# The fifth pair's queries: a buffer freed by moving the first pair's rest, an earlier load, a later scaling

## The chip, the cores and the metric

The kernel runs on one core of a Trainium2 chip. The metric is the device time in microseconds. Before, six runs gave a median of 1515.28 us (1513.14 to 1515.76).

The engines are named as in the profile: PE is TensorE (matmuls; PEld are its weight loads), DVE is VectorE, ACT is ScalarE, POOL is GpSimd, SP is SyncE, whose queue here issues nearly all loads. Each engine works through its own queue in order and waits on semaphores for the others.

## The reference

An attention with a threshold, for 8 batches of 8 heads with 576 positions and a head size of 64, followed by a SwiGLU block over the 4608 tokens that come out of it:

```python
scores = scale * np.matmul(q, k.transpose(0, 1, 3, 2))       # scale = 1/8
thresh = np.max(scores, axis=-1, keepdims=True) - tau
scores = np.where(scores >= thresh, scores, -1000000000.0)
scores = scores - np.max(scores, axis=-1, keepdims=True)
attn = np.exp(scores)
attn = attn / (np.sum(attn, axis=-1, keepdims=True) + 1e-09)
attn_out = np.matmul(attn, v)                                # q, k, v: (8, 8, 576, 64)
x = attn_out.transpose(0, 2, 1, 3).reshape(8 * 576, 512)
g = x @ w_gate                                               # w_gate, w_val: (512, 1536)
silu = g * (1.0 / (1.0 + np.exp(-g)))
out = (silu * (x @ w_val)) @ w_out                           # w_out: (1536, 512)
```

All is in float32.

## The kernel before

**Pairs, tiles and segments.** Two heads make a pair; a batch has four pairs (NP = 4), the whole input 32. A pair's 576 queries are cut into four tiles of 128 and one of 64. Pair and tile numbers in the code count from 0: the "fifth pair" is pair 4, the first of the second batch. The main loop (L856 to L923) runs over segments. The first four segments are the first two tiles of pairs 0 to 3 (tiles one to eight of the run). The next four are the three remaining tiles of pairs 3, 0, 1 and 2 (tiles nine to twenty). From then on each segment is one whole pair in another layout ("halved"). In the loop `n` is the segment and `x` the tile in it, so `n == NP - 1` holds the seventh and the eighth tile, and `n == NP` begins with the ninth.

**One tile.** `scores` (L316) is a generator that a tile steps through: score matmuls on PE (L343, or L348 for the short tile), the row maximum on DVE (L370), threshold and exponential on ACT (L376, L377), masking with the row sum on DVE (L381), sum and reciprocal `ri` (L405, L406), and, from the third tile of a pair on, the division by the sum: the first head on ACT (L389), the second on POOL (L387). `flip` (L431) then turns the tile before on PE, one head after the other (L447; both scaled heads are needed), and ACT copies the two heads out of PSUM (L455) and the end piece (L460). `attend_tile` (L463) multiplies with the values (L475, L479), copied by ACT (L481). Between these steps `fill` issues matmuls of the SwiGLU block (`pg` and `pv`, L537) as far as rows of it are ready; the order of all this is written out by hand. The PSUM tiles of `flip`, `attend_tile` and the SwiGLU block share four buffers, so a new one waits for the copy out of an older one.

**Weights.** The weights come in pieces through a few places: two DMA issues on SP (L185), a split in two by ACT (L196, L197), three steps on DVE (L203, L207, L210) and a sum on POOL (L212). One piece goes through per tile; the load of the next into a place waits until the piece there is split and joined.

**Queries and keys.** `load_qk` (L231) loads a pair with four DMA issues for the keys and four for the queries. For pairs 1, 2 and 3 the raw data have places of their own in larger buffers (`places_`, L235); pair 0 and all pairs from 4 on use the tiles `qraw` and `kraw` of a pool with a single buffer each (L242). For pairs 0 to 3 the first 256 queries (QA) are loaded at once, and the remaining 320 later, by `load_rest` (L272), into the same raw tile; each load is followed by a scaling by `scl` on POOL (L253), which the main loop takes out of the deque `scales` at a tile of its choice (L914 to L920). From pair 4 on, `load_qk` issues eight loads on SP and the scaling of all 576 queries at once (L278 to L280). The loop calls it for the next pair in the first tile of each segment from the fifth on (L886), for pair 4 thus in the ninth tile.

**Transposes.** `prepare` (L804) turns a pair's raw keys and queries with DVE. The rests of pairs 0, 1 and 2 are turned in the ninth, tenth and eleventh tile (L902 to L904). Pair 0's rest is read there out of the very `qraw` that pair 4's queries take next, so pair 4's first load waits for that transpose.

`xall` holds the rows for the SwiGLU block (five parts of XW = 1024 columns, XB = 5) and behind them two parts of 768, `hs2` and `hs3`, used from the third unit of that block on. Pair 3's raw keys and queries lie in the first 1152 columns behind XB * XW.

Of the kernel before, what the change touches and what calls it, by code (L numbers as in the profile page):

```python
# [14 lines left out]
ALU = mybir.AluOpType  # L15
# [4 lines left out]
def kernel(  # L20
# [30 lines left out]
    nc = tc.nc  # L51
    P = 128
    B, H, S, D = q.shape
    NP = H // 2
# [3 lines left out]
    G = 32  # L58
    NG = P // G
    NJ = S // G  # L60
# [7 lines left out]
    XB = 5  # L68
# [5 lines left out]
    QA = TA * P  # L74
# [20 lines left out]
    scl = const.tile([P, 1], F32, name="scl")  # L95
# [21 lines left out]
    def run_idle(n):  # L117
        ps = ps_f.tile([P, 512], F32, name="idle", tag="psf")[:, 0:TC]
        for _ in range(n):
            nc.tensor.matmul(ps, ones[:, 0:P], ones, start=True, stop=True)  # L120
# [9 lines left out]
    XW, HW = NCC * TC, NF2 * P  # L130
    xall = const.tile([P, XB * XW + 2 * HW], F32, name="xall")
# [84 lines left out]
    def need(n):  # L216
        while len(joined) < n:
            fetch_weights(2)
            if not split:
                split_weights()  # L220
            join_weights()
            split_weights()
# [8 lines left out]
    def load_qk(i):  # L231
        b, hp_ = divmod(i, NP)
        tiles = {}

        places_ = {1: extra[:, 0:2 * S], 2: extra[:, 2 * S:4 * S], 3: xall[:, XB * XW:XB * XW + 2 * S]}  # L235
        srcs = {"q": (q, "(j r) (e d) -> e r j d"),
                "k": (k, "(j r) (e d) -> e r j d" if b == 0 else "(r j) (e d) -> e r j d")}
        for x, name in enumerate("qk"):
            if i in places_:
                tiles[name] = places_[i][:, x * S:(x + 1) * S].rearrange("p (j d) -> p j d", d=G)  # L240
            else:
                tiles[name] = ld.tile([P, NJ, G], F32, name=f"{name}raw")  # L242
        raws = [tiles[name].rearrange("p j d -> p (j d)") for name in "qk"]

        def load(name, js, queues):
            src, order = srcs[name]
            for g in range(NG):
                h, e = divmod(g, 2)
                queues[g // 2].dma_start(out=tiles[name][g * G:(g + 1) * G, js],
                                         in_=src[b, 2 * hp_ + h].rearrange(order, r=G, d=G)[e][:, js])  # L250

        def scale(cs):
            nc.gpsimd.tensor_scalar(out=raws[0][:, cs], in0=raws[0][:, cs], scalar1=scl, scalar2=None, op0=ALU.mult)  # L253

        if i < NP:

            queues = [nc.sync, nc.scalar if i < 2 else nc.sync]
            load("k", slice(0, NJ), queues)
            if i == 0:
                nc.scalar.dma_start(out=tau_s, in_=tau.partition_broadcast(P))  # L260
            load("q", slice(0, QA // G), queues)
            if i == 0:
                nc.vector.tensor_scalar(out=scl, in0=tau_s, scalar1=0.0, scalar2=SCALE, op0=ALU.is_ge, op1=ALU.mult)
                nc.vector.tensor_scalar(out=cap, in0=tau_s, scalar1=0.0, scalar2=2e38, op0=ALU.is_ge, op1=ALU.mult)
                nc.vector.tensor_scalar(out=cap, in0=cap, scalar1=-1e38, scalar2=None, op0=ALU.add)
                nc.vector.scalar_tensor_tensor(out=cut, in0=tau_s, scalar=-1.0, in1=cap, op0=ALU.mult, op1=ALU.min)
            elif i == 1:
                scale(slice(0, QA))
            else:
                scales.append(lambda: scale(slice(0, QA)))  # L270

            def load_rest():  # L272
                load("q", slice(QA // G, NJ), [nc.sync] * 2)
                scales.append(lambda: scale(slice(QA, S)))

            more_loads.append(load_rest)
        else:
            for name in "qk":  # L278
                load(name, slice(0, NJ), [nc.sync] * 2)
            scale(slice(0, S))  # L280
        return raws

    def load_v(seg):
# [446 lines left out]
    def fill(n):  # L730

        credit[0] += n
        while credit[0] > 0:
            c = next(pieces)
            left[0] -= c
            credit[0] = credit[0] - c if c else 0
            if not c:
                return 0
        return 1
# [18 lines left out]
    rest = list(range(TA, NT + 1))  # L758
# [36 lines left out]
    raws = {}  # L795
    more_loads, scales = deque(), deque()
    kept = {}
    later = []

    def fetch_qk(i):  # L800
        if i < NPAIR and i not in raws and i not in kept:
            raws[i] = load_qk(i)

    def prepare(seg):  # L804

        i = seg["i"]
        if i in kept:
            seg.update(kept[i])
            return
        qr, kr = raws[i]  # L810
        kept[i] = None
        qT = qkp.tile([P, S], F32, name="qT")
        if i < NP:
            kT = pall[:, 4 + i, :]
            rest = flat[:, i * (S - QA):(i + 1) * (S - QA)]
            nc.vector.transpose(out=kT, in_=kr)
            if i == 0:
                nc.vector.tensor_scalar(out=qr[:, 0:QA], in0=qr[:, 0:QA], scalar1=scl, scalar2=None, op0=ALU.mult)
            nc.vector.transpose(out=qT[:, 0:QA], in_=qr[:, 0:QA])

            later.append((rest, qr[:, QA:S]))
            if i == NP - 1:
                to, fr = later.pop()
                nc.vector.transpose(out=to, in_=fr)
            kept[i] = {"kT": kT, "qT": rest, "q0": QA}
        else:
            kT = qkp.tile([P, S], F32, name="kT")
            nc.vector.transpose(out=kT, in_=kr)
            nc.vector.transpose(out=qT, in_=qr)
        seg.update(kT=kT, qT=qT, q0=0)  # L830

    def give(n):
        for u in segs[n]["gives"]:
            ready.append(u)
            left[0] += cost(u)
        gains[n] = (gains[n][0], 0)

    run_idle(6)
    fetch_qk(0)
    prepare(segs[0])  # L840
    fetch_qk(1)

# [13 lines left out]
    for n, seg in enumerate(segs):  # L856
        if NP <= n < 2 * NP:
            seg["v"] = segs[seg["i"]]["v"]
        for x, t in enumerate(seg["tiles"]):
            go = scores(seg, t)  # L860
            next(go)
            if not n and not x:
                run_idle(6)
            next(last, None)
            attends = prev is not None and x == 1
            products = iter(())
            attend_tile()
            next(go)
            next(last, None)
            flip()  # L870
            if n == NP and x == 0:
                attend_tile()
                give(n - 1)
            if n == 2 * NP and x == 1:
                give(n - 1)
            if attends and n > 2 * NP:
                if prev["i"] % NP == 0:
                    need(NW)
                    start_batch(prev["i"] // NP)
                products = attend(prev)  # L880
            part = pace(n, x) / 2
            more = len(split)
            if n or x:
                split_weights()
                fetch_weights(2)
            if x == 0 and n >= NP:  # L886
                fetch_qk(seg["i"] + 1)
            next(go)
            double = t == NT and NP <= n < NP + 2
            if more and not double:  # L890
                join_weights()
            fill(part)
            next(go)
            fill(part)
            if double:

                join_weights(2)
                split_weights()
                fetch_weights(2)
            gates()  # L900
            last = go
            if n == NP and later:  # L902
                to, fr = later.pop(0)
                nc.vector.transpose(out=to, in_=fr)  # L904
            if attends and n > 2 * NP:
                next(products)
                next(products)
                give(n - 1)
            if attends and seg["halved"]:
                load_v(seg)  # L910
            if x == 0 and 0 < n < NP - 1:
                load_v(segs[n + 1])
                more_loads.popleft()()
            if n == 0 and x == 1 or n == 1:  # L914
                scales.popleft()()
            elif n == NP - 2 and x == 1:
                more_loads.popleft()()
                scales.popleft()()
            elif n == NP - 1:
                scales.popleft()()  # L920
            if x == len(seg["tiles"]) - 2 and n + 1 < len(segs):
                prepare(segs[n + 1])
        prev = seg  # L923
# [42 lines left out]
```

## Time and profile before

| | us |
|---|---|
| median of six runs | 1515.28 |
| lowest, highest run | 1513.14, 1515.76 |
| the profiled execution | 1514.41 |
| its span, first to last instruction | 1512.6 |
| PE busy in 75 to 160 us of the span | 81.23 of 85 |
| PE busy in 160 to 200 us | 33.11 of 40 |
| DVE busy in 160 to 200 us | 36.35 of 40 |
| PE busy in 200 to 1400 us | 1194.75 of 1200 |

The span is what one profiled execution shows from its first to its last instruction; the time of that execution lies 1.81 us above it. The change touches the stretch of the seventh to the eleventh tile, some 48 to 85 us after the start: the ninth tile's scores come at 53.4, the tenth's at 64.3, the eleventh's at 75.1. A list of waits tells which instruction stood idle for which other; a timeline gives each engine's instructions in order of time, with the idle time before one in brackets. PE's granted clock is shown per window; its mean over the span is 0.998.

### The profile page before, as it was taken

The numbers are of one execution on the slowest core, as the hardware profiler recorded it, in microseconds if no ns is written. First come the engines' busy times: TensorE is split into PE (matmuls) and PEld (weight loads), VectorE is DVE, ScalarE is ACT, GpSimd is POOL, SyncE is SP. The second block draws the span as 40 slices with busy tenths as digits, with TensorE's granted clock in tenths as the row PEclk, the third lists the DMA queues.
The fourth block names the chain that finished last, engine by engine and source line by source line (L and its number), as shares of the span: only waits on it lengthen the run. The fifth ranks groups of instructions, "written<-read, shape, count | busy, mean of one in ns | idle before, by whom it ended". The sixth has DMA issues, their size and how long they took to land. (4 is left out here: it accounts for less than half of the span.)

```text
span 1512.6 us, 31511 instructions
## 1 busy us (share of the span) xinstructions
PE 1485.2 (98%) x11808; PEld 1125.4 (74%) x11808; DVE 997.0 (66%) x3040; ACT 726.6 (48%) x2158; POOL 642.2 (42%) x640
## 2 busy tenths in 40 slices
PE   9899899999999999999999999999999999999998
PEld 6677564477777777787777777777777777888887
DVE  7878988777777777747667666776666767512212
ACT  6777665555455545434545445454544554311110
POOL 2545543367454535336444444543545353500000
PEclk9999999999999999999999999999999999999999
DMA  8642411211212111112111111112110120000000
GB/s 175 170 142 94 96 33 40 53 33 32 47 33 47 33 28 29 41 28 46 33 29 28 24 46 33 46 33 47 33 38 12 45 48 16 1 14 1 15 15 15
DMA packets 177064, 66.93 MB, mean 44 GB/s; under 512 B 159888, under 2 KB 159888, under 8 KB 176912
## 3 DMA queue, kind: packets, MB, share of 16 engines
q1 hardware_dynamic: 170880, 56.62, 16.4%
q0 software_dynamic: 2432, 7.87, 1.4%
q8 instruction: 94, 1.54, 0.4%
q10 hardware_dynamic: 3600, 0.43, 0.2%
q14 instruction: 58, 0.48, 0.1%
HBM read 55.44 MB, written 9.44 MB: 43 GB/s over the span
## 5 line engine op out<-in xcount | busy, mean ns | idle before, releaser
L387 POOL TENSOR_SCALAR pall<-pall,ri 128x288 f32<-128x288 f32 (+1 forms) x260 | 265.0, 1029 | 337.8 <-DVE ri L397 314.8
L537 PE MATMUL pv<-xall,wgv 128*128 128x256 f32 x1728 | 405.1, 383 | 1.6 <-ACT pall L455 1.3
L537 PE MATMUL pg<-xall,wgv 128*128 128x256 f32 x1728 | 403.6, 383 | 0.2 <-ACT pall L455 0.2
L537 PEld LDWEIGHTS pv<-xall,wgv 128*128 128x128 f32 x1728 | 324.8, 190 | 67.5 <-issue 22.3
L537 PEld LDWEIGHTS pg<-xall,wgv 128*128 128x128 f32 x1728 | 323.8, 190 | 65.5 <-issue 22.0
L358 DVE TENSOR_REDUCE mx<-sc 128x2 f32<-128x576 f32 x252 | 180.5, 751 | 237.6 <-PE sc L335 236.8
L381 DVE SCALAR_TENSOR_TENSOR pall<-sc,th,pall 128x288 f32<-128x288 f32 (+1 forms) x540 | 258.1, 528 | 31.1 <-ACT pall L377 31.1
L377 ACT ACTIVATE pall<-sc,nm 128x288 f32<-128x288 f32 (+1 forms) x540 | 236.4, 510 | 0.6
L373 ACT ACTIVATE th<-nm,cut 128x4 f32<-128x4 f32 (+1 forms) x140 | 41.6, 297 | 383.8 <-DVE nm L362 383.8
L569 POOL TENSOR_TENSOR ht<-ht,gt 128x512 f32<-128x512 f32 x84 | 107.0, 1274 | 194.0 <-DVE ht L557 109.8
L426 DVE STREAM_TRANSPOSE pall<-pall 128x576 f32<-128x576 f32 x252 | 181.4, 754 | 2.8 <-POOL pall L387 2.8
L635 PE MATMUL po<-wo,ht 128*128 128x256 f32 x768 | 177.5, 381 | 0.0
L335 PE MATMUL sc<-kT,qT 64*32 64x288 f32 x4032 | 158.5, 412 | 11.7 <-DVE pall L381 10.5
L635 PEld LDWEIGHTS po<-wo,ht 128*128 128x128 f32 x768 | 144.6, 190 | 26.4 <-issue 6.0
L557 DVE SCALAR_TENSOR_TENSOR ht<-tn,pv 128x512 f32<-128x512 f32 x102 | 69.9, 685 | 132.3 <-PE pv L537 119.1
L389 ACT ACTIVATE pall<-pall,ri 128x288 f32<-128x288 f32 (+1 forms) x264 | 132.9, 553 | 0.0
L311 ACT COPY sums<-sums 32x4 f32<-32x4 f32 (+1 forms) x560 | 108.4, 194 | 49.8 <-DVE pall L381 38.6
L550 ACT ACTIVATE tn<-pg 128x512 f32<-128x512 f32 x108 | 64.8, 600 | 139.8 <-PE pg L537 133.0
L501 PE MATMUL xa<-pall,vall 64*64 64x288 f32 x2016 | 128.7, 405 | 0.0
L335 PEld LDWEIGHTS sc<-kT,qT 64*32 64x32 f32 x4032 | 58.9, 106 | 89.4 <-issue 61.3
L501 PEld LDWEIGHTS xa<-pall,vall 64*64 64x64 f32 x2016 | 74.4, 133 | 50.7 <-ACT sums L311 3.6
L653 POOL TENSOR_TENSOR ht<-ht,xall 128x256 f32<-128x256 f32 x48 | 34.1, 729 | 156.3 <-PE po L635 155.1
(110 smaller groups left out, 1339.1 us busy)
## 6 DMA issues: line engine op xcount, KB each, us to landing
vall<-in_v_dram SPq DMA_DIRECT2D x112, 144.0 KB, 3.3
kraw<-in_k_dram SPq DMA_DIRECT2D x114, 72.0 KB, 2.7
qraw<-in_q_dram SPq DMA_DIRECT2D x112, 72.0 KB, 2.4
out_dram<-ob POOLq DMA_DIRECT2D x28, 256.0 KB, 2.6
wo<-in_moe_w_gate_dram SPq DMA_DIRECT2D x16, 384.0 KB, 3.6
wo<-in_moe_w_val_dram SPq DMA_DIRECT2D x16, 384.0 KB, 4.4
xall<-in_moe_w_out_dram SPq DMA_DIRECT2D x5, 768.0 KB, 4.6
wo<-in_moe_w_out_dram SPq DMA_DIRECT2D x3, 768.0 KB, 4.7
```

Of the source, the lines that this page charges most:

```text
L311: nc.scalar.copy(out, in_[:, :, 0])
L335: nc.tensor.matmul(ps[g * G:(g + 1) * G, h, 0:SH], qT[hs, col + a * G:col + (a + 1) * G], kT[hs, c * SH:(c + 1) * SH], start=True, stop=True)
L358: nc.vector.tensor_reduce(out=mx[:, 2 * x:2 * x + 2, 0], in_=tile_[:, :, 0:SH], axis=AX.X, op=ALU.max, negate=True)
L377: nc.scalar.activation(ps[x], scs[x], AF.Exp, bias=nm[:, x:x + 1])
L381: nc.vector.scalar_tensor_tensor(out=ps[x], in0=scs[x], scalar=th[:, x:x + 1], in1=ps[x], op0=ALU.is_ge, op1=ALU.mult, accum_out=sm[:, x, ...
L387: nc.gpsimd.tensor_scalar(out=ps[x], in0=ps[x], scalar1=ri[:, x:x + 1], scalar2=None, op0=ALU.mult)
L389: nc.scalar.activation(ps[x], ps[x], AF.Copy, scale=ri[:, x:x + 1])
L426: nc.vector.transpose(out=p, in_=p)
L501: nc.tensor.matmul(xa[a][h * D:(h + 1) * D, at:at + n * G].rearrange("d (i q) -> d i q", q=G), vr[rs, h, j, :], p[rs, lo:lo + n, j, :], st ...
L537: nc.tensor.matmul(ps[:, i], wgv[:, mat, c, (f + i) * P:(f + i + 1) * P], x[:, c, cs], start=(c == 0), stop=(c == NCC - 1))
L569: eng.tensor_tensor(out=hts[x], in0=hts[x], in1=gt, op=ALU.mult)
L635: nc.tensor.matmul(ps, h(f), w[:, f, :], start=(f == 0), stop=(f == NF2 - 1))
```

## The change

`load` gets an optional target, so that the rest of the queries can land elsewhere than in the raw tile; `scale` takes the data instead of a range of columns. Pair 0's rest gets 320 columns of `xall` behind pair 3's raw data (columns 1152 to 1472 behind XB * XW); the rests of the other pairs stay in their raw tiles. `raws[i]` gets a third entry, the rest, which `prepare` hands on to the transposes. Pair 4 no longer scales its queries where it loads them, but puts the scaling into `scales`. The load of pair 4 is called in the seventh tile (`n == NP - 1`; the second call in the eighth finds it done, as does the former call in the ninth), and the scaling is taken out in the tenth (`n == NP`, `x == 1`).

```diff
-        def load(name, js, queues):
+        def load(name, js, queues, to=None):
             src, order = srcs[name]
+            to = tiles[name][:, js] if to is None else to
             for g in range(NG):
                 h, e = divmod(g, 2)
-                queues[g // 2].dma_start(out=tiles[name][g * G:(g + 1) * G, js],
+                queues[g // 2].dma_start(out=to[g * G:(g + 1) * G],
                                          in_=src[b, 2 * hp_ + h].rearrange(order, r=G, d=G)[e][:, js])
 
-        def scale(cs):
-            nc.gpsimd.tensor_scalar(out=raws[0][:, cs], in0=raws[0][:, cs], scalar1=scl, scalar2=None, op0=ALU.mult)
+        def scale(x):
+            nc.gpsimd.tensor_scalar(out=x, in0=x, scalar1=scl, scalar2=None, op0=ALU.mult)
...
             elif i == 1:
-                scale(slice(0, QA))
+                scale(raws[0][:, 0:QA])
             else:
-                scales.append(lambda: scale(slice(0, QA)))
+                scales.append(lambda: scale(raws[0][:, 0:QA]))
+
+            own = xall[:, XB * XW + 2 * S:XB * XW + 3 * S - QA] if i == 0 else raws[0][:, QA:S]
+            raws.append(own)
 
             def load_rest():
-                load("q", slice(QA // G, NJ), [nc.sync] * 2)
-                scales.append(lambda: scale(slice(QA, S)))
+                load("q", slice(QA // G, NJ), [nc.sync] * 2, own.rearrange("p (j d) -> p j d", d=G))
+                scales.append(lambda: scale(own))
 
             more_loads.append(load_rest)
         else:
             for name in "qk":
                 load(name, slice(0, NJ), [nc.sync] * 2)
-            scale(slice(0, S))
+            if i == NP:
+                scales.append(lambda: scale(raws[0]))
+            else:
+                scale(raws[0])
         return raws
...
-        qr, kr = raws[i]
+        qr, kr = raws[i][0:2]
...
-            later.append((rest, qr[:, QA:S]))
+            later.append((rest, raws[i][2]))
...
             elif n == NP - 1:
                 scales.popleft()()
+                fetch_qk(NP)
+            elif n == NP and x == 1:
+                scales.popleft()()
             if x == len(seg["tiles"]) - 2 and n + 1 < len(segs):
                 prepare(segs[n + 1])
```

In the built program PE's and ACT's queues are the same instructions in the same order, and so is DVE's, but for the place from which it turns pair 0's rest. On SP the eight loads of pair 4 stand directly behind the weight piece of the seventh tile, ahead of two weight pieces that stood before them. On POOL pair 4's scaling stands behind the tenth tile's L212 instead of ahead of the ninth tile's L387.

## The prediction

> **What bounds the kernel now.** I read first the busy times of the page, for the engine whose work fills the span.
>
> ```profile
> PE 1485.2 (98%) x11808; PEld 1125.4 (74%) x11808; DVE 997.0 (66%) x3040; ACT 726.6 (48%) x2158; POOL 642.2 (42%) x640
> ```
>
> PE is busy for 1485.2 of 1512.6 us. The change neither adds nor removes a matmul, so it can win only out of the 27.4 us in which PE stands still, and out of time in which PE runs at a lower clock. The list of waits for the whole span has one large single wait of PE, 3.4 us, and the list for 60 to 80 us, which holds the stretch that the change touches, has what stands in front of it (columns: who waited for whom, total us, times, longest).
>
> ```profile
> POOL qraw L253 <- DMA qraw<-in_q_dram: 7.2, 1, 7.2
> ...
> PE tp L447 <- POOL pall L387: 3.4, 1, 3.4
> ```
>
> The timeline of each engine there (start us, duration, engine, line, work, then the idle time before it in brackets) gives the chain. DVE, SP, POOL and PE in this order:
>
> ```profile
> 61.68 0.51 DVE L904 STREAM_TRANSPOSE pall<-qraw 128x320 f32<-128x320 f32 x1
> ...
> 62.22 1.95 SPq L249 DMA_DIRECT2D qraw<-in_q_dram  x4
> 64.21 2.70 SPq L249 DMA_DIRECT2D kraw<-in_k_dram  x4
> 67.01 0.56 SPq L185 DMA_DIRECT2D wo<-in_moe_w_gate_dram  x1
> ...
> 57.97 1.08 POOL L253 TENSOR_SCALAR extra<-extra,scl 128x320 f32<-128x320 f32 x1
> 66.20 1.72 POOL L253 TENSOR_SCALAR qraw<-qraw,scl 128x576 f32<-128x576 f32 x1 [7.16 <-DMA qraw<-in_q_dram]
> 67.91 1.72 POOL L387 TENSOR_SCALAR pall<-pall,ri 128x576 f32<-128x576 f32 x1
> ...
> 65.62 0.66 PE L447 MATMUL tp<-pall 128*128 128x128 f32 x4
> 69.68 1.04 PE L447 MATMUL tp<-pall 128*128 128x128 f32 x4 [3.40 <-POOL pall L387]
> ...
> 71.58 3.57 PE L537 MATMUL pv<-xall,wgv 128*128 128x256 f32 x12
> 75.08 1.19 PE L348 MATMUL sc<-pall 64*64 64x288 f32 x8
> ```
>
> The fifth pair's queries land in the buffer that still holds the rest of the first pair's, so SP holds their load until DVE has transposed that rest (61.68 + 0.51 = 62.19). GpSimd's scaling of them stands in its queue ahead of the ninth tile's scaling (L387) and waits 7.16 us for the load; L387 ends at 69.6, and only then may PE turn the second head (L447). The last view is the windows: length, busy times by engine, then the granted clock (1.00 is full), DMA share, GB/s.
>
> ```profile
> 66.00:68.00 2.00, 0.28 (x3) 0.04 (x1) 1.67 (x3) 1.61 (x4) 1.79 (x2) 1.00 0.70 109
> 68.00:70.00 2.00, 0.32 (x2) 0.32 (x3) 1.93 (x7) 0.60 (x2) 2.00 (x2) 0.95 1.02 246
> 70.00:72.00 2.00, 2.00 (x8) 1.74 (x7) 1.97 (x2) 1.19 (x3) 2.00 (x2) 0.50 0.47 182
> 72.00:74.00 2.00, 2.00 (x8) 1.67 (x7) 1.92 (x3) 2.00 (x4) 2.00 (x2) 0.70 0.00 0
> 74.00:76.00 2.00, 2.00 (x14) 1.14 (x12) 0.00 (x0) 0.91 (x2) 1.50 (x1) 1.00 0.60 154
> ```
>
> After the stall PE gets half its clock: the missing shares 0.05, 0.50 and 0.30 of 2 us each, doubled, are 3.4 us at half rate. So the stall costs twice.
>
> **The change, part by part.**
>
> *Rest of the first pair's queries in a place of its own.* The four loads of 128x320, the 1.08 us scaling and the 0.51 us transpose stay, with the same sizes and at the same places in SP's, GpSimd's and DVE's queues; only the address differs. Cost 0. It frees the fifth pair's buffer: its earlier readers, the first pair's transposes, were done before 8 us.
>
> *Fifth pair's load in the seventh tile.* Eight DMA issues move forward on SP, past two weight pieces of two issues each (at 50.77 and 56.09 us now), to behind the piece of 46.91 to 47.77. Eight such issues took 1.95 + 2.70 = 4.65 us here, 5.77 us in another place (at 24.38), and four took 3.93 us at worst (at 39.70), so 4.7 to 7.9 us: SP is free again at 52.4 to 55.6. The first weight piece is then 1.7 to 4.9 us later, the second (due at 56.09) not at all. They land 3.6 to 4.5 us after issue, by 60.1 at the latest; ScalarE splits the first not before 69 us, so some 9 us cover it, and without that cover each us would cost a us, since the split holds ScalarE's queue and the PSUM copies in it. The later pieces gain: the one now issued at 67.01 no longer waits behind the eight. The queries land by about 60 us and are scaled after 73.
>
> *Queries scaled in the tenth tile.* The 1.72 us instruction leaves the place ahead of L387 and goes behind the tenth tile's weight sum (L212). There GpSimd idles 8.02 us (75.5 to 83.5) before the next sum, so it costs nothing; were that gap gone, 1.72 us would fall on the weight sums. Its reader, DVE's transpose, comes at 142.7.
>
> *What L387 does now.* GpSimd is free at 59.05, `ri` of the ninth tile is ready at 59.72 (reciprocal at 59.55 for 0.17), so L387 runs from about 59.8 to 61.6, and the second head can be turned as soon as PE has turned the first, at 66.28. DVE's weight steps beside it get slower: with L387 running at 96.3 they took 1.02 and 0.95 us against 0.54 and 0.56, some 0.9 us, inside the 3.41 us that DVE then idles before 65.60.
>
> *What is late next.* From 66.28 PE runs: eight transposes take 1.09 to 1.16 us elsewhere, so four 0.56; the end piece 0.11; two pg matmuls at 3.29/14 = 0.235 us each, 0.47. That is 67.4. The next tile, pv, takes over the PSUM buffer of the first head, which ScalarE empties only after the tenth tile's exponentials:
>
> ```profile
> 68.02 0.58 ACT L455 COPY pall<-tp 128x512 f32<-128x512 f32 x1
> ```
>
> These hang on scores that are no earlier than before, so pv starts at 68.60 + 0.1 = 68.7: 1.3 us of the stall come back as a wait on ScalarE. A gap of 1.32 us at 111.59 left the clock at 1.00 (mean of 100 to 120 us), so I take full rate: 12 x 0.235 = 2.82, and the scores of the eleventh tile start at 71.5 instead of 75.08.
>
> Sum at this place: 3.40 (stall) + 1.45 (half clock: 69.68 to 75.08 is 5.40, the same work at full rate 0.56 + 0.11 + 14 x 0.235 = 3.96) - 1.27 (new wait, 67.42 to 68.7) = 3.58 us. Bounds of the unseen wait: 0, if ScalarE copies the first head before the exponentials, which its order excludes; at most 1.85, if pv waited for the second copy (68.60 + 0.58, + 0.1). So the local gain is 3.0 to 4.85; the copy that is first in order is the likeliest.
>
> *Does it last?* After 75 us DVE waits for PE's scores, PE for ScalarE's copies, and ScalarE for PE's products, so all of them move together. Between 160 and 200 DVE is busy 36.35 of 40 us and PE waits for it (longest 2.59 us), but that stretch starts from scores that PE gives at 147 and 153.6. From 200 to 1400 PE is busy 1194.75 of 1200 us. No ScalarE wait on a DMA stands in 60 to 160 us, so no transfer fixes a time there. I keep all of it.
>
> *The clock, rule against row.* The Trainium skill, "TensorE: Matmul & The Clock Gate", section "What's actually happening", says that PE falls to half rate after a wholly idle window of about 3.4 us, on a free-running count. Here a gap of 2.59 us at 166.7 also brought the drop (0.70 in 168 to 170, 0.50 in 170 to 172), so a part of a window is enough, and the measurement decides. By the rule a 3.40 us gap hardly ever fills a window, the drop would be rare, and the gain would be about 2.1 us, time 1513.2; by the rows it is 3.58.
>
> **Sum.** The profiled execution took 1514.41 us, 1512.6 of span and 1.81 around it; 0.87 below the median of 1515.28. Less 3.58 it is 1510.8; from the median, 1511.7 us. That is 0.24% faster.
>
> **Rivals.** About 0.2%, 3.03 us here, is what a measurement can tell from no change.
>
> *Half the gain, 1513.2.* The drop of the clock is not in all runs of before (they spread from 1513.14 to 1515.76). Then 3.40 - 1.27 = 2.1 us are won. For it: the spread. Against it: four of six runs lie at 1515.2 or more. Within 0.2%.
>
> *The gain is lost again, 1515.3.* DVE's stretch from 160 to 200 would have to start from something that doesn't move. For it: DVE is the limit there. Against it: its start hangs on PE's scores, and no transfer is in the chain.
>
> *Slower, 1519.* The eight loads hold SP, and the weight piece behind them comes too late for ScalarE. Price: one us for each us past the cover. To end 3.7 us slower it must eat 9 us of cover, the 3.6 us won and 3.7 more, that is SP must be held until about 72 us, more than 20 us for eight issues; the worst row gives 7.9.
>
> *The change doesn't do what it says.* If a hidden wait kept the load behind the transpose, GpSimd would still be free for L387, since the scaling has moved: the gain would stand, 1511.7, and its chance is in the forecast's.
>
> **Chances.** Forecast (gain 3.0 to 4.9) 0.64, half the gain 0.22, lost 0.10, slower 0.04. Of the forecast's own width a little falls under 3.03: faster 0.62, same 0.34, slower 0.04. The forecast alone gives 1515.28 - 4.85 = 1510.4 to 1512.3. The lower end is 1509.5: 1511.0, the middle of the forecast's better half, less 1.45 for a run in which the drop of the clock at 168 stays out as well. The upper end, 1514.0, takes in half the gain and leaves out lost and slower.
>
> **What would show it.** Right: L387 of the ninth tile near 59.8; no GpSimd wait on the queries; PE's gap before the second L447 gone, one of about 1.3 before pv; clock 1.00 from 64 to 76; the eleventh tile's scores near 71.5; DVE's busy stretch 3.6 us earlier; the load's issues from about 48. Wrong: a ScalarE wait on a weight DMA near 69, a clock below 1.00 in that stretch, or later waits of PE on DVE that grow by what was won.

## The result, and the profile after

The changed kernel takes 1510.87 us (median of 18 runs, 1510.57 to 1512.97); the kernel before, run on the same chips, 1515.38 us (36 runs, 1513.14 to 1517.07). The ratio is 0.9975 [0.9969, 0.9982], so 3.8 us less (2.7 to 4.7). The profiled execution took 1510.88 us with a span of 1509.1, 3.5 us less than the span of before.

First the timeline of the changed kernel for 45 to 84 us, in the columns of the prediction (start, duration, engine, line, work, idle time before it in brackets). The engines follow one another: SP, POOL, DVE, ACT, PE. L387 is now L395, L447 is L455, L455 is L463, L537 is L545, L348 is L356.

```profile
47.62 2.40 SPq L250 DMA_DIRECT2D qraw<-in_q_dram  x4
50.06 4.63 SPq L250 DMA_DIRECT2D kraw<-in_k_dram  x4
54.80 0.56 SPq L185 DMA_DIRECT2D wo<-in_moe_w_gate_dram  x1
...
58.09 1.09 POOL L254 TENSOR_SCALAR extra<-extra,scl 128x320 f32<-128x320 f32 x1
60.02 1.88 POOL L395 TENSOR_SCALAR pall<-pall,ri 128x576 f32<-128x576 f32 x1 [0.83 <-DVE ri L414]
...
73.91 1.73 POOL L254 TENSOR_SCALAR qraw<-qraw,scl 128x576 f32<-128x576 f32 x1
80.01 4.16 POOL L212 TENSOR_TENSOR wgv<-wgv,extra 128x768 uint32<-128x768 uint32 x2 [4.37 <-DVE wgv L210]
...
59.77 0.54 DVE L203 TENSOR_SCALAR wgv<-wgv 128x768 f32<-128x768 f32 x1
60.34 0.98 DVE L207 TENSOR_SCALAR wgv<-wgv 128x768 uint32<-128x768 uint32 x1
...
68.15 1.07 ACT L463 COPY pall<-tp 128x512 f32<-128x512 f32 x2
...
69.25 0.96 ACT L196 ACTIVATE wgv<-wo 128x768 f32<-128x768 f32 x1
...
65.75 1.09 PE L455 MATMUL tp<-pall 128*128 128x128 f32 x8
...
66.78 0.60 PE L545 MATMUL pg<-xall,wgv 128*128 128x256 f32 x2
68.78 2.86 PE L545 MATMUL pv<-xall,wgv 128*128 128x256 f32 x12 [1.40 <-ACT pall L463]
71.57 1.19 PE L356 MATMUL sc<-pall 64*64 64x288 f32 x8
```

GpSimd no longer stands for 7.16 us before the queries. It starts the ninth tile's scaling (L395) at 60.02, as soon as `ri` is ready, and is done at 61.90. PE turns both heads without a break (one group of eight at 65.75, where before it was four, 3.40 us of idleness, and four). What is left of the stall is 1.40 us before pv, for which the profile names ScalarE's first copy. The eleventh tile's scores start 3.51 us earlier, at 71.57.

The windows of the changed kernel (length, busy times of PE, PEld, DVE, ACT, POOL, then granted clock, DMA share, GB/s):

```profile
66.00:68.00 2.00, 1.38 (x11) 0.98 (x9) 1.67 (x3) 1.48 (x4) 0.00 (x0) 1.00 0.05 18
68.00:70.00 2.00, 1.22 (x6) 1.09 (x7) 1.90 (x8) 2.00 (x5) 0.33 (x1) 1.00 0.00 0
70.00:72.00 2.00, 2.00 (x12) 1.44 (x12) 1.97 (x3) 2.00 (x4) 1.55 (x1) 1.00 0.00 0
```

In these six us, where before the clock fell to 0.50, it is 1.00. The distance that was won stays: the halved tiles' scores stand at 143.51, 165.77 and 197.02 us, against 147.02, 169.28 and 200.53 before, 3.51 us each time.

### The profile page after: what moved, and what is told of

It is laid out like the page before. It is cut to its first block, busy times and chain, and to the rows that moved or that the text cites. A ratio compares the mean times of both kernels' runs of the same rounds, so it can differ in the third digit from the quotient of the medians.

```text
span 1509.1 us, 31512 instructions
## 1 busy us (share of the span) xinstructions
PE 1483.9 (98%) x11808; PEld 1124.2 (74%) x11808; DVE 995.7 (66%) x3040; ACT 727.2 (48%) x2158; POOL 643.2 (43%) x640
## 5 line engine op out<-in xcount | busy, mean ns | idle before, releaser
L395 POOL TENSOR_SCALAR pall<-pall,ri 128x288 f32<-128x288 f32 (+1 forms) x260 | 265.7, 1031 | 343.7 <-DVE ri L405 317.2
L545 PE MATMUL pv<-xall,wgv 128*128 128x256 f32 x1728 | 404.6, 383 | 3.0 <-ACT pall L463 2.7
L545 PE MATMUL pg<-xall,wgv 128*128 128x256 f32 x1728 | 403.2, 382 | 0.2 <-ACT pall L463 0.2
L545 PEld LDWEIGHTS pv<-xall,wgv 128*128 128x128 f32 x1728 | 324.1, 190 | 68.9 <-issue 22.3
L545 PEld LDWEIGHTS pg<-xall,wgv 128*128 128x128 f32 x1728 | 323.5, 190 | 65.5 <-issue 22.0
```

Of the source, the lines that this page charges most:

```text
L395: nc.gpsimd.tensor_scalar(out=ps[x], in0=ps[x], scalar1=ri[:, x:x + 1], scalar2=None, op0=ALU.mult)
L545: nc.tensor.matmul(ps[:, i], wgv[:, mat, c, (f + i) * P:(f + i + 1) * P], x[:, c, cs], start=(c == 0), stop=(c == NCC - 1))
```

## The experiments

Each was timed against the kernel before; the first four shared 24 runs of it (median 1514.98 us), and the next two 19 (median 1514.78 us).

### The scaling alone

The kernel before, with the shared buffer and the late load as they were, but the scaling of pair 4's queries goes into the deque and is taken out in the tenth tile.

```diff
-            scale(slice(0, S))
+            if i == NP:
+                scales.append(lambda: scale(slice(0, S)))
+            else:
+                scale(slice(0, S))
...
+            elif n == NP and x == 1:
+                scales.popleft()()
```

> The kernel before, with only one part of the change: the scaling of the fifth pair's queries leaves its place ahead of the ninth tile's L387 and stands in the tenth tile. The buffer is still shared and the load still waits for the transpose. Theory (the whole gain is GpSimd's queue: L387 stood behind an instruction that waited for a load): L387 starts near 60.0 us, PE's 3.40 us stall is gone, the 1.4 us wait before pv is there, and the time is that of the changed kernel, 0.9975 of before (0.997 to 0.998), although the eight loads are still issued from 62.2 on. Rival (place and early load carry the gain, through SP's queue and the weight piece issued at 67.01): the ratio stays above 0.999.

Measured: 1511.04 us (9 runs, 1510.78 to 1513.43), ratio 0.9976 [0.9966, 0.9986]. Timeline of this kernel, SP, POOL, PE (its L390 is L387 of before, its L540 is L537, its L351 is L348):

```profile
62.79 1.95 SPq L249 DMA_DIRECT2D qraw<-in_q_dram  x4
64.79 3.21 SPq L249 DMA_DIRECT2D kraw<-in_k_dram  x4
68.10 0.56 SPq L185 DMA_DIRECT2D wo<-in_moe_w_gate_dram  x1
...
60.04 1.88 POOL L390 TENSOR_SCALAR pall<-pall,ri 128x576 f32<-128x576 f32 x1 [0.84 <-DVE ri L409]
...
68.80 2.86 PE L540 MATMUL pv<-xall,wgv 128*128 128x256 f32 x12 [1.40 <-ACT pall L458]
71.59 1.19 PE L351 MATMUL sc<-pall 64*64 64x288 f32 x8
```

The load still waits for the transpose, as before, and is issued from 62.79. Yet GpSimd scales at 60.04 and the scores come at 71.59, 0.02 us from the whole change. Moving the waiting instruction out of its place ahead of L387 is enough.

### The place alone

The changed kernel without its other two parts: pair 4 is loaded in the ninth tile, and its queries scaled there at once. Only the buffer is free earlier.

```diff
-            if i == NP:
-                scales.append(lambda: scale(raws[0]))
-            else:
-                scale(raws[0])
+            scale(raws[0])
...
-                fetch_qk(NP)
-            elif n == NP and x == 1:
-                scales.popleft()()
```

> The changed kernel with only the other part: the first pair's rest has its own place, but the fifth pair is loaded in the ninth tile and scaled at once, ahead of L387, as before. Theory: what counts is only that L387 ends before PE has turned the first head (66.4 us). SP is free from 57.0, so the queries land at about 61.8, the scaling ends at 63.6 and L387 at 65.4, 1.0 us in time: no stall of PE, ratio to before 0.9975 as for the whole change. Rival (the order on GpSimd is what matters): L387 still comes too late, PE's wait for it is over 1 us, ratio 0.9985 to 1.000.

Measured: 1511.04 us (9 runs, 1510.76 to 1512.79), ratio 0.9973 [0.9963, 0.9982]. Timeline of this kernel, SP, POOL, PE:

```profile
56.95 2.35 SPq L250 DMA_DIRECT2D qraw<-in_q_dram  x4
...
62.71 1.72 POOL L254 TENSOR_SCALAR qraw<-qraw,scl 128x576 f32<-128x576 f32 x1 [3.65 <-DMA qraw<-in_q_dram]
64.42 1.73 POOL L392 TENSOR_SCALAR pall<-pall,ri 128x576 f32<-128x576 f32 x1
...
65.63 1.23 PE L452 MATMUL tp<-pall 128*128 128x128 f32 x8
...
71.45 1.19 PE L353 MATMUL sc<-pall 64*64 64x288 f32 x8
```

GpSimd still waits 3.65 us for the queries, with L392 (L387 of before) behind it. That scaling ends at 64.42 + 1.73 = 66.15, 0.75 us later than expected and just as PE comes to the second head: PE's eight transposes take 1.23 us instead of 1.09. All the remaining wait of GpSimd costs PE is some 0.14 us, and none of it is left at 71.45. So the place alone suffices, and the later scaling alone does, and together they bring nothing more: what counts is that the ninth tile's scaling is done by about 66 us. The earlier load, with the scaling left ahead of L387, was not run.

### ScalarE's copies first

By the profile, the 1.40 us before pv is a wait for ScalarE's first copy, which stands behind the tenth tile's exponentials. Here the changed kernel turns the ninth tile ahead of the tenth's exponentials, so that the copies come first.

```diff
             attend_tile()
+            if n == NP and x == 1:
+                flip()
             next(go)
             next(last, None)
-            flip()
+            if n != NP or x != 1:
+                flip()
```

> The changed kernel; in the tenth tile the two heads are turned, and ScalarE's copies of them issued, ahead of that tile's exponentials instead of behind them. Theory (the remaining 1.40 us of PE before pv is a wait for ScalarE's first copy, which stands behind exponentials that wait for DVE): pv starts near 67.3 and 1.3 to 1.4 us are won on top, time 1509.5, ratio to before 0.9966 (0.9960 to 0.9970). Rival (the copies only push the exponentials back by 1.2 us, and DVE and the next tile's turn pay for it): ratio 0.9975 or above, with a new wait of PE near 72 to 75 us.

Measured: 1510.66 us (6 runs, 1510.57 to 1510.76), ratio 0.9970 [0.9959, 0.9981]. ACT's and PE's timeline in this kernel, then a line of DVE in the changed kernel:

```profile
74.17 0.29 ACT L384 ACTIVATE th<-nm,cut 128x1 f32<-128x1 f32 x1 [1.33 <-DVE nm L378]
...
75.00 1.06 ACT L463 COPY pall<-tp 128x512 f32<-128x512 f32 x2
...
67.20 2.77 PE L545 MATMUL pv<-xall,wgv 128*128 128x256 f32 x12
69.90 1.19 PE L356 MATMUL sc<-pall 64*64 64x288 f32 x8
...
75.62 2.43 PE L545 MATMUL pg<-xall,wgv 128*128 128x256 f32 x10 [1.15 <-ACT pall L463]
77.98 1.36 PE L351 MATMUL sc<-pall 64*128 64x288 f32 x10
```

```profile
72.80 0.76 DVE L378 TENSOR_REDUCE nm<-sc 128x1 f32<-128x576 f32 x1 [0.41 <-PE sc L356]
```

The wait before pv is gone, so ScalarE's order did cause it, and the eleventh tile's scores are 1.67 us earlier. But the tenth tile's exponentials start 1.07 us later (67.79 against 66.72), and DVE's work behind them is late in its turn: DVE takes up the eleventh tile's row maximum (L378) only at 73.42, though its scores came early, against 72.80 in the changed kernel, where it had waited 0.41 us for them. ScalarE stands 1.33 us for that maximum, and its copies behind it make PE wait 1.15 us one tile further on. The twelfth tile's scores start at 77.98, against 78.23 in the changed kernel, so 0.25 us is left. The expected 1509.5 us was not reached; the time doesn't differ measurably from the changed kernel's. The ratio alone can't tell the theory from its rival, but the trace shows what the rival had named: the copies push the exponentials back, and DVE and the next tile pay for it.

### The stall without the clock

The kernel before, with seven matmuls of 128x256 put between the two heads' turns in the ninth tile. Their result is overwritten unread; PE is busy in the stall, but has to wait as before.

```diff
             tp = ps_f.tile([P, 512], F32, name="tp", tag="psf")
+            if (seg["i"], t, h) == (NP - 1, TA, 1):
+                for _ in range(7):
+                    nc.tensor.matmul(tp[:, 0:TC], ident, pall[:, 4, 0:TC], start=True, stop=True)
```

> The kernel before, with seven matmuls of 128x256 that nobody reads put between the turns of the ninth tile's two heads, where PE stalls: 7 x 2 x 0.235 = 3.29 us of work in a stall of 3.40. Theory (the stall costs a second time, because PE's clock is halved for 3.4 us after it): the stall stays, L447 of the second head still starts near 69.7, the granted clock stays at 1.00, the scores of the eleventh tile come at about 73.7 instead of 75.08, and the time falls by 1.45 us to a ratio of 0.9990 (0.9985 to 0.9995). Rival (the slow matmuls after the stall have another cause, or runs without a profile don't have the drop): ratio 1.000.

Measured: 1513.28 us (11 runs, 1512.64 to 1514.44), ratio 0.9987 [0.9978, 0.9996]. PE's timeline (L445 is the seven unread matmuls, L450 is L447 of before), then a window of this kernel:

```profile
65.99 3.19 PE L445 MATMUL tp<-pall 128*128 128x256 f32 x14
69.83 0.66 PE L450 MATMUL tp<-pall 128*128 128x128 f32 x4 [0.65 <-POOL pall L387]
...
73.55 1.19 PE L348 MATMUL sc<-pall 64*64 64x288 f32 x8
```

```profile
70.00:72.00 2.00, 2.00 (x13) 1.82 (x13) 1.97 (x2) 1.42 (x3) 2.00 (x2) 1.00 0.68 269
```

The second head is turned no earlier (69.83, against 69.68 before), so the stall itself is not shortened. The clock stays at 1.00, and from the second head's turn to the scores it is 3.72 us (69.83 to 73.55), where it was 5.40 before (69.68 to 75.08). By that the clock alone is worth 1.68 us here; the prediction had 1.45. The scores are 1.53 us earlier, since the head itself came 0.15 later. The ratio agrees, but is not sharp: 2.0 us less (0.6 to 3.3).

### The load twice, and four times

The rival "slower" said that the eight issues on SP make a weight piece late. Here the changed kernel loads the same queries and keys twice (or four times) into the same place, which lengthens the hold of SP and adds those transfers.

```diff
-            for name in "qk":
+            for name in "qk" * (2 if i == NP else 1):
```

> The changed kernel with the fifth pair's eight loads issued twice, one set behind the other into the same place: 16 issues ahead of the weight piece. Theory (the loads' hold on SP is covered, since ScalarE splits that weight piece only at 69.25 us): the first set took 47.62 to 54.69, a second takes 4.7 to 7 us more, so the piece is issued at 59.5 to 61.7 and lands by 66; nothing waits for it, ratio to before 0.9975, as the changed kernel. Rival (more transfers and a longer held queue cost at once): above 0.9985.

> The same with the loads issued four times, 32 issues. Theory (past the cover each us of hold costs a us): the piece is issued between 69 and 76 us and lands at 73 to 80; ScalarE waits for it from 69.25 on, for the first time in a kernel here, for 4 to 11 us, PE with it; the time rises by as much over the changed kernel, so 1515 to 1522, ratio to before 1.000 to 1.005. Rival (later pieces have enough reserve to take it up): ratio under 0.9985.

Measured: twice, 1511.97 us (10 runs, 1510.61 to 1513.96), ratio 0.9980 [0.9970, 0.9989]; four times, 1516.72 us (10 runs, 1515.88 to 1519.37), ratio 1.0011 [1.0002, 1.0020]. SP and PE with the load twice:

```profile
60.22 0.55 SPq L185 DMA_DIRECT2D wo<-in_moe_w_gate_dram  x1
...
71.46 1.19 PE L356 MATMUL sc<-pall 64*64 64x288 f32 x8
```

SP, ACT and PE with the load four times:

```profile
66.58 3.36 SPq L250 DMA_DIRECT2D kraw<-in_k_dram  x4
70.05 0.56 SPq L185 DMA_DIRECT2D wo<-in_moe_w_gate_dram  x1
...
74.87 0.89 ACT L196 ACTIVATE wgv<-wo 128x768 f32<-128x768 f32 x1 [4.67 <-DMA wo<-in_moe_w_val_dram]
...
77.36 0.66 PE L455 MATMUL tp<-pall 128*128 128x128 f32 x4 [2.41 <-ACT pall L397]
```

With 16 issues the piece that follows is issued at 60.22 instead of 54.80, and nothing in this stretch moves: the scores stand at 71.46. The median is 1.1 us above the changed kernel's, but the intervals of the ratios overlap, the fastest four runs (1510.61 to 1511.02) equal the changed kernel's, and what the profiled execution lost (1513.37 us) it lost after 100 us, with the clock at half from 109.4 to 116.2. With 32 issues SP is held from 47.30 to 69.94, ScalarE waits 4.67 us for the weights, and PE 2.41 us for ScalarE. The twelfth tile's scores come at 82.13, where 78.23 in the changed kernel and a start 0.81 us later would make it 79.04: 3.09 us lost for 4.67 of waiting. The rest of this profile's 6.0 us of span against the changed kernel lies with the late start and a stretch at half clock from 113 to 121 us. The median is 5.9 us above the changed kernel's, inside the expected 4 to 11; yet even the fastest of the ten runs (1515.88) is 5.3 above the changed kernel's fastest, so more than the 3.09 us is lost in each of them, and one profile can't say where. The mechanism of the rival "slower" is real: a hold of 12.2 us (47.88 to 60.11, with the load twice) cost nothing in this stretch, one of 22.6 did. The change holds SP for 7.1 us.

### Both kernels once more

Each kernel was profiled once more, on one chip.

> The kernel before once more, for a second profile. Theory (the runs differ by which of PE's gaps bring the drop of the clock: about 67, 111 and 168 us): the stall of 3.40 us and a drop behind it are there again; the time of the execution goes with the number of drops in its profile, 1513.2 with one, 1514.4 with two, 1515.5 or more with three. Rival: the spread has nothing to do with the clock's drops.

> The changed kernel once more, for a second profile. Theory: no drop near 67 us; with one drop elsewhere 1510.8, with two 1511.9 to 1513.0. Rival: the spread has nothing to do with the clock's drops.

Measured: 1515.45 us for the kernel before, 1511.34 for the changed one. POOL and PE in the second profile of the kernel before:

```profile
66.65 1.72 POOL L253 TENSOR_SCALAR qraw<-qraw,scl 128x576 f32<-128x576 f32 x1 [7.46 <-DMA qraw<-in_q_dram]
68.35 2.13 POOL L387 TENSOR_SCALAR pall<-pall,ri 128x576 f32<-128x576 f32 x1
...
70.53 1.12 PE L447 MATMUL tp<-pall 128*128 128x128 f32 x4 [4.12 <-POOL pall L387]
75.69 1.19 PE L348 MATMUL sc<-pall 64*64 64x288 f32 x8
```

The queries landed later here, L387 took 2.13 us instead of 1.72, and the stall was 4.12 us, not 3.40. From the tenth tile's scores (64.46) to the eleventh's it is 11.23 us, against 10.75 in the first profile and 7.12 in the changed kernel's. The gain at this place is thus 3.6 us in one pair of profiles and 4.1 in the other. In the second profile of the changed kernel PE's next gap, 107 to 108 us, was followed by half clock, which it was not in the first:

```profile
108.19 2.41 PE L351 MATMUL sc<-pall 64*128 64x288 f32 x10 [1.31 <-DVE pall L389]
```

```profile
110.00:112.00 2.00, 2.00 (x23) 1.24 (x21) 1.97 (x3) 0.94 (x2) 1.43 (x2) 0.50 0.00 0
```

The second profile of before has half clock after this gap as well (1.29 us there), so it is no effect of the change.

Neither count of drops gave the expected time. The second profile of before has two drops, behind the stall and near 115 us, and took 1515.45 us where 1514.4 was expected; that of the changed kernel has two, near 110 and near 168 us, and took 1511.34 instead of 1511.9 to 1513.0. What a drop costs depends on where it falls. The first profile of before has one near 168 us, the second has none there. PE in the first and in the second profile, then a window of the second (its timeline was taken up to 178 us, so its last group is cut short there):

```profile
169.28 2.17 PE L335 MATMUL sc<-kT,qT 64*32 64x288 f32 x32 [2.59 <-DVE pall L381]
...
176.90 0.72 PE L335 MATMUL sc<-kT,qT 64*32 64x288 f32 x16 [0.54 <-DVE pall L381]
```

```profile
170.27 0.72 PE L335 MATMUL sc<-kT,qT 64*32 64x288 f32 x16 [2.60 <-DVE pall L381]
...
177.89 0.48 PE L335 MATMUL sc<-kT,qT 64*32 64x288 f32 x8 [1.51 <-DVE pall L381]
```

```profile
170.00:172.00 2.00, 1.57 (x33) 0.63 (x34) 1.97 (x8) 1.58 (x7) 0.00 (x0) 1.00 0.00 0
```

The second stays 0.99 us behind the first on both sides of the drop (0.50 in 170 to 172 us of the first): at half clock PE only waits less for DVE afterwards, 0.54 us instead of 1.51. So the drop near 168 us cost nothing.

## Why the prediction was right

*The place, at no cost.* This was right, and with the place alone the whole gain is there.

*The load.* The eight issues took 7.07 us (47.62 to 54.69) with the gap between them (4.7 to 7.9 expected). The weight piece behind them came 4.03 us later (54.80 against 50.77; expected 1.7 to 4.9), and ScalarE took it at 69.25 without a wait. The cover of about 9 us was right too. With the load four times ScalarE began the split 4.82 us after the piece's first issue (70.05 to 74.87); a piece issued at 54.80 would by that be there at 59.6, an estimated 9.6 us ahead of 69.25. The load twice used 5.4 us of it (60.22 against 54.80) and lost nothing.

*The scaling.* This was right: it takes 1.73 us at 73.91 and delays no weight sum. The gap it stands in is shorter than before, 6.10 us instead of 8.02, and 4.37 of it stay idle.

*L387.* Expected 59.8 to 61.6, found 60.02 to 61.90: the instruction took 1.88 us, not 1.72, beside DVE's weight steps. Of these only the second was slowed as expected (0.98 us); the first, begun 0.25 us ahead of L387, took 0.54 and not 1.02. The row at 96.3 us had overstated it, in a place where it costs nothing.

*The new wait.* 1.40 us instead of 1.27; pv at 68.78 (68.7 expected), scores at 71.57 (71.5). That the wait came from ScalarE's order was right. The copies-first kernel adds that another order doesn't win it: the wait returns one tile later, by way of DVE.

*The clock.* The drop behind the stall is shown by the kernel with the unread matmuls. It costs 1.68 us there, a little more than the 1.45 of the sum, since the work at full rate takes 3.72 us and not 3.96. That a gap of 1.3 us leaves the clock at 1.00 was read from one execution and was too much to conclude: a gap of 1.31 us at 107 us did bring the drop in the second profile of the changed kernel. The 1.40 us before pv brought none in either of its profiles. The lower end of the range took another 1.45 us for a run without the drop at 168; that term was wrong, since the two profiles of before, one with that drop and one without, show that it cost nothing.

*It lasts.* This is shown: the gain is 3.51 us at 71.57, at 143.51, at 165.77 and at 197.02.

*The sum.* 3.40 + 1.45 - 1.27 = 3.58 was the forecast; the pair of profiles gives 3.51 (3.53 of the executions' times), the comparison of many runs 3.8 (2.7 to 4.7), and the two medians lie 4.5 apart. Counted from the tenth tile's scores the profiles give 3.63; the clock was put 0.23 us too low and the new wait 0.13 too low, which partly cancel, so the close agreement is in part luck. What the first term missed is that the stall is not the same in each execution of before: 3.40 us in one, 4.12 in the other, since it ends with a transfer and with an instruction of varying length. The profiled execution was one of the faster ones, 0.87 us below the median. How the stall is spread over all runs was not measured, so the last 0.7 us between the paired comparison and the medians stay open.

*The rivals.* "Half the gain" assumed that the clock does not drop in all runs of before; both of its profiles show the drop at this place, and the times leave no room for 2.1 us. The rule of the Trainium skill, "TensorE: Matmul & The Clock Gate", section "What's actually happening", by which a 3.40 us gap would hardly ever bring it, does not hold here: that gap brought it, and gaps of 1.29 to 1.32 us did in six of ten profiles. "Lost again" is refuted by the distance that stays, "slower" by the split at 69.25, which waits for nothing; with the load four times its price was not one us for each us of waiting, but 3.09 us for 4.67. "Doesn't do what it says" had its time right: with the load behind the transpose as before, the time was the same 1511.0.

## What to carry to other kernels

An instruction that waits for a transfer holds up all that is behind it in an in-order queue; look for what stands behind it and whom that serves, and move it, or bring the transfer forward: here moving it was enough, and so was freeing the buffer that the transfer waited for, and doing both brought nothing more. Price a stall of PE with the time at half clock after it (here 3.40 + 1.7 us), and subtract the wait that was hidden under it (1.40 us); where PE waits for another engine anyway, half clock can cost nothing, as near 168 us here. Changing a second engine's order need not win a short wait: here what was put back held up a third engine, and the wait came back a tile later.

## What the hardware showed

- PE's clock fell to 0.50 after gaps of 3.40 and 4.12 us in the two profiles that have them, after one of 2.59 to 2.61 us near 168 us in seven of ten profiles, and after one of 1.29 to 1.32 us near 110 us in six of ten; in the others the same gaps left it at 1.00. A drop lasts some 3.4 us; in the profiles of the place alone and of the load twice it lasted two such lengths, from 109.4 to 116.2 us, and in that of the load four times as well. One length near 110 us moved the scores at 143.51 by 0.32 us (143.95 in the second profile of the changed kernel, which starts 0.12 later), two lengths by 1.99 (145.38 with the place alone, which starts 0.12 earlier). The changed kernel's runs lie at 1510.6 to 1510.9, 1511.8 to 1512.2 and 1512.7 to 1513.0. The distance of the last group, some 2 us, would fit two lengths; no profile was taken of a run in the last two groups, and for the middle one no cause is shown.
- In the kernel with the load four times, the four issues for the keys took 4.44 us the first time, 2.59 us each of the next two times and 3.36 us the last, though the same bytes go to the same place. Why was not tried.
